# Six PSUM banks for sums and one buffer for scores, in a fused attention and gated feed-forward kernel

## The chip, the core and the metric

The kernel runs on one core of a Trainium2 chip. The metric is the device time in microseconds; the kernel before takes 428.95 us, the median of 3 runs (428.2 to 429.21). The profile is that of one execution, with a span of 426.9 us.

The engines are named as in the profile: PE is TensorE's matmul, PEld its weight load, DVE is VectorE, ACT is ScalarE, POOL is GpSimd (here it issues loads), SP is SyncE (here it issues stores and transposing transfers).

## The reference

Eight batches of twelve heads, 448 positions, 64 numbers a head. Attention squares the relu of the scores in place of a softmax; its output goes through a feed-forward block with a gate.

```python
batch, n_heads, seq, head_dim = (8, 12, 448, 64)
scores = q @ k.T / sqrt(head_dim)
attn = np.maximum(scores, 0.0) ** 2 / seq
x = (attn @ v)                      # heads side by side: 3584 x 768
g = x @ w_gate                      # 768 x 1536
gelu = 0.5 * g * (1.0 + erf(g / sqrt(2)))
val = x @ w_val                     # 768 x 1536
out = (gelu * val) @ w_out          # 1536 x 768
```

## The kernel before

All matmuls are bf16 and use a quarter of the array: 64 rows by 64 columns. The program speaks of two row halves, `PE0` (lower, rows 0 to 63) and `PE1` (upper, rows 64 to 127). Both columns of a half get one matmul each at the same time, and both halves work side by side. A line of the profile that names L159 is one of these matmuls, whichever part of the kernel it serves; the tiles tell them apart: `sp` are scores, `ff` are sums.

PSUM is shared out in two pools. A score buffer takes two banks, one for each row half; a sum takes one.

```python
    SB = 2
    FB = 4
    ...
    psS = ctx.enter_context(tc.tile_pool(name="psS", bufs=SB, space=bass.MemoryType.PSUM))
    psF = ctx.enter_context(tc.tile_pool(name="psF", bufs=FB, space=bass.MemoryType.PSUM))
```

**Sums.** There are three kinds, and all take turns in the four banks: gate and value sums (`ff<-xT,wg`, `ff<-xT,wv`; 6 steps in each half, of two matmuls of 448 columns), output sums (`ff<-wo,uT`; 12 steps in each half, 384 columns), and value products of the attention (`ff<-attnT,v`). The lower half does its steps first, then the upper half adds its own to the same bank, while the lower half is at the next sum. `wait_lower` makes the upper half wait for the last matmul of the lower.

```python
    def add_gate_value(at, b, fc, g):
        ...
        def emit(r, dc):
            if not box:
                box[0] = new_bank(done)
            if r == 1 and dc == 0:
                wait_lower(box)
            for j in range(2):
                ins = mm(box[0][HALF[j], 0:S], w[HALF[r], dc, o + P * j:o + P * (j + 1)],
                         xT[b][HALF[r], dc, :], r, j, r == 0 and dc == 0, r == 1 and dc == KC - 1)
            box[1] = ins
        ...
        ops = [[Op(f"PE{r}", GS, lambda r=r, dc=dc: emit(r, dc),
                   [w12_op[i][g], x_op[b, dc], *(ring_dep() if r == 0 and dc == 0 else ())], lag=0.24)
                for dc in range(KC)] for r in range(2)]
```

A bank is free again when its reader is done: for a gate sum the gelu on ScalarE (`gel`), for a value sum the product on VectorE (`uT`), for an output sum the copy on ScalarE (`osb`), for an attention product the copy on VectorE (`xT`). `ring` holds the readers, and `ring_dep` names the one of four sums ago.

```python
    def ring_dep():
        return [ring[-FB]] if len(ring) >= FB else []
```

**Scores.** A batch has 21 score units. A unit is a pair of matmuls in each half (of 448 columns; the units at a group's middle take two pairs of 224); its relu on ScalarE reads both banks at once (128 x 896), and VectorE squares the result. `units` holds the relus, and a unit waits for the one of two units ago.

```python
        have = [*have, *units[-SB:1 - SB]]
        ops = [[Op(f"PE{j}", 0.095 if tail else 0.189, lambda j=j, pr=pr: emit(j, pr), have, lag=0.24)
                for pr in prs] for j in range(2)]
        ...
        relu = Op("ACT", 0.8, emit_relu, [ops[0][-1], ops[1][-1], *sq_list[-4:-3]], lag=0.18, prio=2)
        ...
        units.append(relu)
```

**The planner.** The kernel decides the order of all instructions while it is built. `run_plan` takes the queues with assumed costs (the second argument of `Op`) and lags and emits, again and again, the operation that can start first. The lower half's order is fixed beforehand: the operations are sorted by their place `at`, which spreads a batch's 21 score units evenly over the feed-forward work of the batch before. The upper half's operations stand in a pool from which the planner takes what is ready.

The batches overlap: while batch b's gate, value and output sums run, the scores and the attention products of a later batch are put between them. The first two batches' queries and keys are transposed on TensorE (the second one's through the score buffers), later ones by transfers.

Of the kernel before, what the change touches and what calls it, by code (L numbers as in the profile page):

```python
# [88 lines left out]
def kernel(  # L89
# [11 lines left out]
    f32 = mybir.dt.float32  # L101
    bf16 = mybir.dt.bfloat16
# [3 lines left out]
    B, H, S, D = q.shape  # L106
# [30 lines left out]
    apool = ctx.enter_context(tc.tile_pool(name="apool", bufs=12))  # L137
    gpool = ctx.enter_context(tc.tile_pool(name="gpool", bufs=3))
    opool = ctx.enter_context(tc.tile_pool(name="opool", bufs=4))
    psS = ctx.enter_context(tc.tile_pool(name="psS", bufs=SB, space=bass.MemoryType.PSUM))  # L140
    psF = ctx.enter_context(tc.tile_pool(name="psF", bufs=FB, space=bass.MemoryType.PSUM))

    ident = const.tile([128, 128], bf16)
# [140 lines left out]
    ring = [warm_op]  # L284

    in_bank = []

    def new_bank(reader, shape=(128, 512), dtype=f32):
        in_bank.append(reader)
        return psF.tile(list(shape), dtype, name="ff", tag="F")  # L290

    def fill(t0, t1):

# [12 lines left out]
    def ring_dep():  # L306
        return [ring[-FB]] if len(ring) >= FB else []
# [14 lines left out]

    att, xT, last_s = {}, {}, {}
    t_op, relu_op, sq_op, o_op, x_op = {}, {}, {}, {}, {}
    units = []

    def add_transposes(at, b, m, rs):

        box = {}

        def emit(r):
            if b == 0:
                t = new_bank(t_op[b, m, r], [128, SC, 2 * P], bf16)
            else:
                if not box:
                    box["S"] = psS.tile([128, 2, 1024], bf16, name="sp", tag="S")
                t = box["S"][:, r, 0:SC * 2 * P].rearrange("d (c x) -> d c x", c=SC)
            box[r] = t
            src = qk16[b].rearrange("p (h c d) -> p h c d", c=SC, d=D)
            for c in range(SC):  # L340
                for j in range(2):
                    nc.tensor.transpose(t[HALF[j], c, :], src[:, 2 * (2 * m + r) + j, c, :],  # L342
                                        ident[:, :], tile_position=(0, P * j))

        def emit_copy(r):
            nc.vector.tensor_copy(by_group(qkT_tile(b))[:, m, :, r, :], box[r])

        last = units[-SB:1 - SB]
        for r in rs:
            have = [*(head_op[b, 2 * m + r, i] for i in range(2)), *(last if b else ring_dep())]  # L350
            lo = Op("PE0", 0.5, lambda r=r: emit(r), have, lag=0.2)
            hi = Op("PE1", 0.4, lambda: None)
            hi.after = lo
            t = t_op[b, m, r] = Op("DVE", 0.54, lambda r=r: emit_copy(r),
                                   [lo, last_s.get(b - 2)], lag=0.2, prio=1)
            DVE.append(t)
            if not b:
                ring.append(t)
            both(at, [(lo, hi)])
        if b:  # L360
            units.append(t)

    def add_scores(at, b, u):


        m, w = divmod(u, SC)
        tail = w == VC - 1
        prs = (2 * m, 2 * m + 1) if tail else (2 * m + (w > VC - 1),)
        cl = w if w < VC else w - VC
        box = {}  # L370

        def emit(j, pr):
            if not box:
                box[0] = psS.tile([128, 2, 512], f32, name="sp", tag="S")
            sp = box[0]
            t = by_group(qkT_tile(b))[HALF[j], m, :, pr % 2, :]
            for i in range(2):
                if tail:
                    n0 = (pr % 2) * S // 2
                    qs = t[:, :, i * P // 2:(i + 1) * P // 2]  # L380
                    mm(sp[HALF[i], j, n0:n0 + S // 2].rearrange("k (c p) -> k c p", c=SC),
                       t[:, VC - 1, HALF[1]], qs, j, i, True, True)
                else:
                    mm(sp[HALF[i], j, 0:S].rearrange("k (c p) -> k c p", c=SC),
                       t[:, cl + i * VC, HALF[1]], t[:, :, HALF[0]], j, i, True, True)

        def emit_relu():
            rl = box[1] = rpool.tile([128, 2, S], bf16, name="rl", tag="rl")
            nc.scalar.activation(rl[:, :, :], box[0][:, :, 0:S], AF.Relu)  # L389

        def emit_sq():
            a = apool.tile([128, 2, S], bf16, name="attnT", tag="attnT")
            for pr in prs:
                att[b, pr, VC - 1 if tail else cl] = a
            nc.vector.tensor_tensor(a[:, :, :], box[1][:, :, :], box[1][:, :, :], op=ALU.mult)  # L395

        if b < EARLY:
            have = [t_op[b, m, pr % 2] for pr in prs]
        else:
            have = tr_op[b, m]  # L400
        have = [*have, *units[-SB:1 - SB]]
        ops = [[Op(f"PE{j}", 0.095 if tail else 0.189, lambda j=j, pr=pr: emit(j, pr), have, lag=0.24)
                for pr in prs] for j in range(2)]
        last_s[b] = ops[1][-1]
        relu = Op("ACT", 0.8, emit_relu, [ops[0][-1], ops[1][-1], *sq_list[-4:-3]], lag=0.18, prio=2)
        n_a = len(sq_list)
        sq = Op("DVE", 0.54, emit_sq, [relu, *att_free[n_a - 12:n_a - 11]] if n_a >= 12 else [relu],
                lag=0.2, prio=2)
        units.append(relu)
        sq_list.append(sq)  # L410
        att_free.append(None)
        for pr in prs:
            sq_op.setdefault((b, pr), []).append((sq, n_a))
            sq_of[b, pr, VC - 1 if tail else cl] = sq
        ACT.append(relu)
        DVE.append(sq)
        both(at, zip(*ops))
# [3 lines left out]
    def add_values(at, b, pr):  # L421
        box = {}

        order = ([0, 3, 1, 2] if pr % 2 else [0, 1, 2, 3], [3, 0, 1, 2])
        last = (b, pr) == (0, NPAIR - 1)

        def emit(i, w):
            if pr == 0 and i == 0 and w == 0:
                xT[b] = xpool.tile([128, KC, S], bf16, name="xT", tag="xT")
            if not box:  # L430
                box[0] = new_bank(x_op[b, pr])
            if (i, w) == (1, VC - 1) or last and (i, w) == (0, 1):
                wait_lower(box)
            for j in range(2):
                o = box[0][HALF[j], 0:S]
                a = att[b, pr, w][HALF[i], j, :]
                if w < VC - 1:
                    ins = mm(o, v16[b][HALF[i], 2 * pr + j, w + i, :], a, i, j,
                       i == 0 and w == 0, i == 1 - last and w == VC - 2)
                else:  # L440
                    ins = mm(o.rearrange("d (c p) -> d c p", c=SC)[:, :, i * P // 2:(i + 1) * P // 2],
                       v16[b][HALF[i], 2 * pr + j, (1 - i) * (VC - 1), :],
                       a[:, (pr % 2) * S // 2:(pr % 2 + 1) * S // 2].rearrange(
                           "k (c p) -> k c p", c=SC), i, j, False, False)
            box[1] = ins

        def emit_copy():
# [2 lines left out]
        sqs = sq_op[b, pr]  # L450
        have = [head_op[b, pr, 2], head_op[b, pr, 3]]
        ops = [[Op(f"PE{i}", 0.189 if w < VC - 1 else 0.095, lambda i=i, w=w: emit(i, w),
                   [*have, sq_of[b, pr, w], *(ring_dep() if i == 0 else ())], lag=0.24)
                for w in order[i]]
               for i in range(2)]
        o_op[b, pr] = ops[1 - last][-1]
# [1 line left out]
            att_free[n_a] = o_op[b, pr]  # L458
        x_op[b, pr] = Op("DVE", 0.54, emit_copy, [o_op[b, pr]], lag=0.2, prio=1)
        DVE.append(x_op[b, pr])  # L460
        ring.append(x_op[b, pr])
        if last:
            ops[1][0].after = ops[0][1]
            for o, p in zip(ops[1], ops[1][1:]):
# [15 lines left out]
    def add_gate_value(at, b, fc, g):  # L480

        i, o = divmod(fc * 128, WCH)
        w = (wg, wv)[g][i]
        box = {}

        def emit(r, dc):
            if not box:
                box[0] = new_bank(done)
            if r == 1 and dc == 0:
                wait_lower(box)  # L490
            for j in range(2):
# [8 lines left out]
        def emit_mult():  # L500
            if fc == 0:
# [2 lines left out]
                uT[b][:, fc, :], gel.pop((b, fc))[:, :], box[0][:, 0:S], op=ALU.mult).ins  # L504

        ops = [[Op(f"PE{r}", GS, lambda r=r, dc=dc: emit(r, dc),
                   [w12_op[i][g], x_op[b, dc], *(ring_dep() if r == 0 and dc == 0 else ())], lag=0.24)
                for dc in range(KC)] for r in range(2)]
        if g == 0:
            done = gel_op[b, fc] = Op("ACT", 0.55, emit_gelu, [ops[1][-1]], lag=0.06, prio=0)  # L510
# [1 line left out]
        else:  # L512
# [3 lines left out]
            if b + 2 < B and b:  # L516
# [7 lines left out]
                elif fc > 6:  # L524
                    h0 = 2 * (fc - 7)
                    load_v(b + 2, h0, h0 + 4, [done])
        ring.append(done)
        if (b, fc) == (0, 0):
            at = [PLACE5 - 0.5 + 0.1 * g] * 3 + [0.01 * g] * 3
        then(at, GS, *ops, done)  # L530
# [1 line left out]
    def add_out(at, t, g):  # L532

        box = {}
        last = 2 * t + 2 == B * SC
        bounds = (0, OGS, OGS + OGS // 2, 2 * OGS) if last else (0, OGS, 2 * OGS)
        cols = slice(bounds[g], bounds[g + 1])
# [3 lines left out]

        def emit(r, fc):
            if not box:
                box[0] = new_bank(cp)
            i, o = divmod(fc, WOG)
            if r == 1 and fc == 0:
                wait_lower(box)
# [11 lines left out]
        def emit_store(j, engine, cols):  # L559
# [3 lines left out]

        ops = [[Op(f"PE{r}", step, lambda r=r, fc=fc: emit(r, fc),
                   [wo_op[fc // WOG], *(u_op[b, fc] for b, _ in chunks),
                    *(ring_dep() if r == 0 and fc == 0 else ())], lag=0.24)
                for fc in range(FC)] for r in range(2)]

        cp = Op("DVE" if last else "ACT", 0.48, emit_copy, [ops[1][-1]], prio=1)
        ring.append(cp)  # L570
        (DVE if last else ACT).append(cp)
        if t == 0:
            load_qk(2, g, H - 4, H, [cp])
# [98 lines left out]


    def emit_filler():
        t = psS.tile([128, 2, 512], f32, name="sp", tag="S")
        for _ in range(2):
            mm(t[HALF[0], 0, 0:P], warm[HALF[0], 0:P], warm[HALF[0], 0:P], 0, 0, True, True)
            mm(t[HALF[1], 0, 0:P], warm[HALF[0], 0:P], warm[HALF[0], 0:P], 0, 1, True, True)
# [68 lines left out]
```

## Time and profile before

| what | from | value |
|---|---|---|
| time, median of 3 | runs | 428.95 us |
| span of the profiled execution | page | 426.9 us |
| one relu of a score unit, 128 x 896 | groups, x168 | 918 ns |
| one gelu, 128 x 448 | groups, x96 | 543 ns |
| one copy of an output sum, 128 x 384, ACT | groups, x54 | 476 ns |
| one product into `uT`, 128 x 448, DVE | groups, x96 | 620 ns |
| one copy into `xT`, 128 x 448, DVE | groups, x48 | 624 ns |
| busy from 167.11 to 266.20 us (99.09 us): DVE, ACT | windows | 53.14, 55.71 us |

The page gives busy time per engine, then the chain of work that ended last, then the costliest groups of instructions with the mean duration of one. The windows give the same busy times for any stretch, with the number of instructions in brackets. The timeline gives the instructions of one engine in order of time, with the start, the length and, in square brackets, the idle time before them. Two things must be kept in mind. The matmuls of four tiles overlap, so PE's busy time is that of their union. And the ends of matmuls are modelled, so their starts are what can be measured.

### The profile page before, as it was taken

To read this page: it belongs to the slowest core of one execution; us is meant where nothing else is said; L and a number is where in the kernel's file an instruction comes from. 1 tells how busy PE (TensorE), PEld (TensorE's weight loads), DVE (VectorE), ACT (ScalarE), POOL (GpSimd) and SP (SyncE) were. 2 spreads that over 40 slices of the span, in tenths; PEclk is the share of its full clock that TensorE was granted. 3 is DMA by queue.
4 is the path that set the end of the run, shared out by engine and by line. 5 is a ranking of instruction groups with operands and counts; after the bars stand their busy time and mean duration, and the time that the engine had idled before them with its cause. 6 is when DMAs were issued, how large, how long until landed. Compare 5 with 4: busy or idle time off the path is not lost.

```text
span 426.9 us, 19600 instructions
## 1 busy us (share of the span) xinstructions
PE 419.6 (98%) x9090; PEld 357.1 (84%) x9090; DVE 212.9 (50%) x347; ACT 223.8 (52%) x320; POOL 73.6 (17%) x120
## 2 busy tenths in 40 slices
PE   8999999989999999999999999999999999999996
PEld 3558769767998889889999988979999988977895
DVE  3976765357643665346643666446643555212201
ACT  4956663466656555555556565555546555322220
POOL 8655401313100131012300122011310000000000
PEclk9999999999999999999999999999999999999999
DMA  7999998999983389545975379645984100120034
GB/s 101 193 199 198 200 209 128 204 128 113 118 137 81 47 114 117 125 76 89 129 121 111 46 96 144 131 63 57 139 141 96 38 4 3 46 71 3 2 77 114
DMA packets 75281, 44.91 MB, mean 105 GB/s; under 512 B 36160, under 2 KB 71744, under 8 KB 75200
## 3 DMA queue, kind: packets, MB, share of 16 engines
q0 software_dynamic: 37152, 24.39, 43.3%
q1 hardware_dynamic: 37888, 19.08, 25.0%
q8 instruction: 71, 1.16, 1.1%
q10 hardware_dynamic: 160, 0.20, 0.1%
q14 instruction: 10, 0.08, 0.1%
HBM read 48.76 MB, written 11.01 MB: 140 GB/s over the span
## 4 chain that ended last, share of the span: by engine, by line
PE 80%; DMA 13%; issue 5%; POOL 1%; DVE 0%; POOLq 0%; DVEq 0%
PE ff L159 74%; PE sp L159 6%; DMA wg<-in_moe_w_gate_dram 4%; DMA wo<-in_moe_w_out_dram 3%; DMA qk<-in_k_dram 3%; DMA qk<-in_q_dram 3%; POOL qk L211 1%; DVE uT L503 0%; POOL v L224 0%; DVE osb L557 0%; POOL ident masks.py:199 0%; POOL ident masks.py:197 0%; DVE qkr L258 0%; POOLq L211 0%; DVEq L258 0%
## 5 line engine op out<-in xcount | busy, mean ns | idle before, releaser
L159 PE MATMUL ff<-xT,wv 64*64 64x448 bf16 x2304 | 216.9, 349 | 1.6 <-issue 1.5
L159 PE MATMUL ff<-xT,wg 64*64 64x448 bf16 x2304 | 217.2, 349 | 0.1
L389 ACT ACTIVATE rl<-sp 128x896 bf16<-128x896 f32 x168 | 152.3, 918 | 97.7 <-PE sp L159 77.2
L159 PE MATMUL ff<-wo,uT 64*64 64x384 bf16 (+1 forms) x2736 | 150.6, 320 | 0.0
L159 PEld LDWEIGHTS <-wv 64*64 64x64 bf16 x2304 | 124.7, 107 | 19.2 <-issue 3.7
L159 PEld LDWEIGHTS <-wg 64*64 64x64 bf16 x2304 | 124.5, 107 | 17.6 <-issue 0.7
L395 DVE TENSOR_TENSOR attnT<-rl 128x896 bf16<-128x896 bf16 x168 | 103.8, 622 | 69.6 <-ACT rl L389 68.3
L159 PEld LDWEIGHTS <-uT 64*64 64x64 bf16 x2736 | 126.8, 107 | 4.4 <-issue 0.3
L159 PE MATMUL sp<-qkT 64*64 64x448 bf16 (+1 forms) x768 | 108.7, 328 | 0.2 <-ACT rl L389 0.2
L503 DVE TENSOR_TENSOR uT<-gel,ff 128x448 bf16<-128x448 bf16 x96 | 59.5, 620 | 73.5 <-PE ff L159 64.6
L159 PE MATMUL ff<-attnT,v 64*64 64x448 bf16 (+1 forms) x768 | 86.1, 326 | 0.1
L498 ACT ACTIVATE gel<-ff 128x448 bf16<-128x448 f32 x96 | 52.1, 543 | 51.7 <-PE ff L159 50.5
L159 PEld LDWEIGHTS <-qkT 64*64 64x64 bf16 x768 | 43.6, 106 | 10.4 <-issue 3.4
L159 PEld LDWEIGHTS <-v 64*64 64x64 bf16 x768 | 45.9, 107 | 5.8 <-issue 1.2
L557 ACT COPY osb<-ff 128x384 f32<-128x384 f32 x54 | 25.7, 476 | 45.6 <-PE ff L159 43.0
L448 DVE TENSOR_SCALAR xT<-ff 128x448 bf16<-128x448 f32 x48 | 29.9, 624 | 33.1 <-PE ff L159 33.1
L211 POOL DMA_DIRECT2D qk<-in_q_dram x25 | 15.5, 621 | 127.6 <-DVE uT L503 106.2
L224 POOL DMA_DIRECT2D v<-in_v_dram x48 | 29.5, 621 | 41.8 <-DVE uT L503 33.0
L211 POOL DMA_DIRECT2D qk<-in_k_dram x25 | 15.4, 615 | 62.2 <-DVE uT L503 54.8
L258 DVE COPY qkr<-qk 128x1792 bf16<-128x1792 bf16 x18 | 19.4, 1079 | 6.6 <-DMA qk<-in_k_dram 6.6
L557 DVE COPY osb<-ff 128x192 f32<-128x192 f32 (+1 forms) x3 | 1.2, 421 | 18.3 <-PE ff L159 18.3
L342 PEld LDWEIGHTS <-qk 128*64 128x64 bf16 x168 | 5.2, 112 | 2.9 <-issue 2.9
(23 smaller groups left out, 42.9 us busy)
## 6 DMA issues: line engine op xcount, KB each, us to landing
out_dram<-osb SPq DMA_DIRECT2D x54, 192.0 KB, 2.8
v<-in_v_dram POOLq DMA_DIRECT2D x48, 128.0 KB, 4.8
qk<-in_q_dram POOLq DMA_DIRECT2D x23, 224.0 KB, 4.5
qk<-in_k_dram POOLq DMA_DIRECT2D x23, 224.0 KB, 4.9
wg<-in_moe_w_gate_dram POOLq DMA_DIRECT2D x6, 384.0 KB, 10.5
wv<-in_moe_w_val_dram POOLq DMA_DIRECT2D x6, 384.0 KB, 11.2
wo<-in_moe_w_out_dram POOLq DMA_DIRECT2D x4, 576.0 KB, 15.3
qkT<-qkr SPq DMA_TRANSPOSE x36, 4.6
```

Source lines behind the costliest of these rows:

```text
L159: return nc.tensor.matmul(o, lhsT, rhs, start=start, stop=stop, tile_position=(P * row, P * col))
L211: op = load(4 * (h1 - h0) * S * D, lambda: nc.gpsimd.dma_start(tile_of().rearrange("p (h x) -> p h x", h=H)[:, h0:h1, :], src[b, h0:h1].re ...
L224: return nc.gpsimd.dma_start(v16[b][HALF[i], h0:h1, :, :], v[b, h0:h1].rearrange("h (p c) d -> p h c d", c=SC)[:, :, c0:c0 + VC, :])
L258: nc.vector.tensor_copy(qkr[b][:, m], qk16[b].rearrange("p (h c d) -> p c h d", c=SC, d=D)[:, :, 4 * m:4 * m + 4])
L342: nc.tensor.transpose(t[HALF[j], c, :], src[:, 2 * (2 * m + r) + j, c, :], ident[:, :], tile_position=(0, P * j))
L389: nc.scalar.activation(rl[:, :, :], box[0][:, :, 0:S], AF.Relu)
L395: nc.vector.tensor_tensor(a[:, :, :], box[1][:, :, :], box[1][:, :, :], op=ALU.mult)
L448: nc.vector.tensor_scalar_mul(xT[b][:, pr, :], box[0][:, 0:S], scalar1=out_scale)
L498: nc.scalar.activation(gel[b, fc][:, :], box[0][:, 0:S], AF.Gelu)
L503: u_op[b, fc].ins = nc.vector.tensor_tensor(uT[b][:, fc, :], gel.pop((b, fc))[:, :], box[0][:, 0:S], op=ALU.mult).ins
L557: cp.ins = (nc.vector.tensor_copy if last else nc.scalar.copy)(osb[t][:, cols], box[0][:, 0:N]).ins
```

## The change

From the end of batch 1's scores on (the second batch), the second score buffer is no longer used for scores: its two banks serve two more sums. All later scores use the one remaining buffer and wait for the relu just before. The sums then take turns in six banks: four in the old pool, then two in the halves of the former score buffer. It is for letting the lower half start a sum without waiting for a bank's reader.

The score pool is split into two pools of one buffer each; `wide` counts the sums since the change of use; `next_bank` says which bank a sum gets and for whom it waits; `next_scores` does so for a score unit.

```diff
-    psS = ctx.enter_context(tc.tile_pool(name="psS", bufs=SB, space=bass.MemoryType.PSUM))
+    psS = [ctx.enter_context(tc.tile_pool(name=f"psS{i}", bufs=1, space=bass.MemoryType.PSUM))
+           for i in range(SB)]
...
-    def new_bank(reader, shape=(128, 512), dtype=f32):
+    units, wide, spare, spare_tile = [], [], [[]], []
+
+    def new_bank(reader, shape=(128, 512), dtype=f32, half=None):
+        if half is not None:
+            if half == 0:
+                spare_tile[:] = [psS[1].tile([128, 2, 512], f32, name="ff", tag="S")]
+            return spare_tile[0][:, half, :]
         in_bank.append(reader)
         return psF.tile(list(shape), dtype, name="ff", tag="F")
+
+    def next_bank():
+
+        n = wide[0] % (FB + 2) - FB if wide else -1
+        if wide:
+            wide[0] += 1
+        if n < 0:
+            return None, ring_dep()
+        if n == 0:
+            spare.append([])
+        return n, spare[-2] if n == 0 else []
+
+    def bank_read(half, reader):
+        (ring if half is None else spare[-1]).append(reader)
+
+    def next_scores():
+
+        if wide:
+            return 0, units[-1:]
+        n = len(units)
+        return n % SB, units[n - SB:n - SB + 1]
+
+    def scores_read(n, reader):
+        units.append(reader)
+        if n == 1:
+            spare[0] = [reader]
...
-        have = [*have, *units[-SB:1 - SB]]
+        have = [*have, *free]
...
-        units.append(relu)
+        scores_read(n, relu)
+        if (b, u) == (EARLY - 1, NU - 1):
+            wide.append(0)
...   (in add_values, add_gate_value and add_out alike)
+        half, free = next_bank()
...
-                box[0] = new_bank(done)
+                box[0] = new_bank(done, half=half)
...
-                   [w12_op[i][g], x_op[b, dc], *(ring_dep() if r == 0 and dc == 0 else ())], lag=0.24)
+                   [w12_op[i][g], x_op[b, dc], *(free if r == 0 and dc == 0 else ())], lag=0.24)
...
-        ring.append(done)
+        bank_read(half, done)
```

More of the change, by code (lines that the diff above doesn't have):

```diff
@@ L324 @@
     t_op, relu_op, sq_op, o_op, x_op = {}, {}, {}, {}, {}
-    units = []
     def add_transposes(at, b, m, rs):
@@ L335, in emit @@
                 if not box:
-                    box["S"] = psS.tile([128, 2, 1024], bf16, name="sp", tag="S")
+                    box["S"] = psS[n].tile([128, 2, 1024], bf16, name="sp", tag="S")
                 t = box["S"][:, r, 0:SC * 2 * P].rearrange("d (c x) -> d c x", c=SC)
@@ L346, in emit_copy @@
             nc.vector.tensor_copy(by_group(qkT_tile(b))[:, m, :, r, :], box[r])
-        last = units[-SB:1 - SB]
+        n, last = next_scores() if b else (0, [])
         for r in rs:
@@ L360, in add_transposes @@
         if b:
-            units.append(t)
+            scores_read(n, t)
     def add_scores(at, b, u):
@@ L370, in add_scores @@
         box = {}
+        n, free = next_scores()
         def emit(j, pr):
             if not box:
-                box[0] = psS.tile([128, 2, 512], f32, name="sp", tag="S")
+                box[0] = psS[n].tile([128, 2, 512], f32, name="sp", tag="S")
             sp = box[0]
@@ L430, in emit @@
             if not box:
-                box[0] = new_bank(x_op[b, pr])
+                box[0] = new_bank(x_op[b, pr], half=half)
             if (i, w) == (1, VC - 1) or last and (i, w) == (0, 1):
@@ L452, in add_values @@
         ops = [[Op(f"PE{i}", 0.189 if w < VC - 1 else 0.095, lambda i=i, w=w: emit(i, w),
-                   [*have, sq_of[b, pr, w], *(ring_dep() if i == 0 else ())], lag=0.24)
+                   [*have, sq_of[b, pr, w], *(free if i == 0 else ())], lag=0.24)
                 for w in order[i]]
@@ L460, in add_values @@
         DVE.append(x_op[b, pr])
-        ring.append(x_op[b, pr])
+        bank_read(half, x_op[b, pr])
         if last:
@@ L484, in add_gate_value @@
         box = {}
+        half, free = next_bank()
         def emit(r, dc):
             if not box:
-                box[0] = new_bank(done)
+                box[0] = new_bank(done, half=half)
             if r == 1 and dc == 0:
@@ L534, in add_out @@
         box = {}
+        half, free = next_bank()
         last = 2 * t + 2 == B * SC
@@ L543, in emit @@
             if not box:
-                box[0] = new_bank(cp)
+                box[0] = new_bank(cp, half=half)
             i, o = divmod(fc, WOG)
@@ L565, in add_out @@
                    [wo_op[fc // WOG], *(u_op[b, fc] for b, _ in chunks),
-                    *(ring_dep() if r == 0 and fc == 0 else ())], lag=0.24)
+                    *(free if r == 0 and fc == 0 else ())], lag=0.24)
                 for fc in range(FC)] for r in range(2)]
         cp = Op("DVE" if last else "ACT", 0.48, emit_copy, [ops[1][-1]], prio=1)
-        ring.append(cp)
+        bank_read(half, cp)
         (DVE if last else ACT).append(cp)
@@ L674, in emit_filler @@
     def emit_filler():
-        t = psS.tile([128, 2, 512], f32, name="sp", tag="S")
+        t = psS[0].tile([128, 2, 512], f32, name="sp", tag="S")
         for _ in range(2):
```

## The prediction

> **What bounds the kernel now.** I read the busy shares first, then the engine's waits, then the chain, then short stretches of it.
>
> The busy shares on the page of the kernel before:
> ```profile
> PE 419.6 (98%) x9090; PEld 357.1 (84%) x9090; DVE 212.9 (50%) x347; ACT 223.8 (52%) x320; POOL 73.6 (17%) x120
> ...
> PEclk9999999999999999999999999999999999999999
> ```
> TensorE is the engine to look at: VectorE and ScalarE are half idle and the clock is full throughout. But "98%" is only a union of matmuls whose ends are modelled. Four 64x64 tiles work side by side, so PE counts as busy when one of its two row halves stands still.
>
> The chain of waits, in order of time (start, length, what):
> ```profile
> 3.13 1.74 POOL qk L211 x3
> ...
> 41.96 13.87 DMA wo<-in_moe_w_out_dram
> 55.88 14.44 issue
> ...
> 167.11 1.95 PE ff L159 x48
> ...
> 266.20 1.95 PE ff L159 x48
> ...
> 365.07 55.63 PE ff L159 x1253
> ```
> Up to about 95 us the chain runs through loads and issue; after that through matmuls alone. The same piece returns at 167.11, 266.20 and 365.07: the steady state repeats every two batches, in 99.1 and 98.9 us.
>
> What would two batches take without a wait? A 448-column matmul of one half follows the one before after 0.189 us, a 384-column one after 0.1625 (from the rule named below; starts in the timeline are 0.19 and 0.16 apart). Per half: 48 gate and value sums x 6 x 0.189 = 54.5; 7 output tiles x 2 sums x 12 x 0.1625 = 27.3; 42 score units, 8.0; 12 value products of the attention, 8.0. Sum 97.7. So **1.2 to 1.4 us per two batches, 0.6 to 0.7 per batch, are lost**; that is all a bank can win in the steady state.
>
> Where? Busy time and count of records in three stretches (stretch; length; PE, PEld, DVE, ACT, POOL busy; clock; DMA):
> ```profile
> 179.65:180.10 0.45, 0.45 (x10) 0.10 (x2) 0.37 (x1) 0.45 (x3) 0.00 (x0) 1.00 0.00 0
> 210.80:211.45 0.65, 0.65 (x16) 0.55 (x12) 0.56 (x1) 0.51 (x1) 0.00 (x0) 1.00 1.27 204
> 386.00:394.00 8.00, 8.00 (x177) 6.08 (x169) 1.86 (x3) 2.17 (x4) 0.00 (x0) 1.00 0.01 2
> ```
> A record counts in every stretch that it touches and lasts 0.35 us. At full rate one expects (length + 0.35) x 4 / 0.189: 177 in the third (there are 177), but 17 in the first, where there are 10. The second, of 384 columns (0.32 us each), should have 24 and has 16. In both, PE is "busy" and one half is idle. ScalarE around the first of them:
> ```profile
> 178.78 0.92 ACT L389 ACTIVATE rl<-sp 128x896 bf16<-128x896 f32 x1 [1.15 <-PE sp L159]
> 179.59 0.47 ACT L557 COPY osb<-ff 128x384 f32<-128x384 f32 x1
> 179.95 0.56 ACT L498 ACTIVATE gel<-ff 128x448 bf16<-128x448 f32 x1
> ```
> The lower half's next value sum starts at 180.12, just after the output copy leaves its bank at 179.59 + 0.47 = 180.06; that copy stood behind the relu of a score unit. This is a wait for a bank.
>
> I put each matmul's start beside the program's order and added up, per row half, the time beyond 0.189 or 0.1625 since the previous start. From 100 to 420 us the lower half idles 4.2 us, the upper 4.8. The pattern repeats: the upper half idles about 0.65 where a batch's gate stage turns into output sums (164, 211, 263, 310, 362 us: 0.63, 0.67, 0.63, 0.67, 0.6), and the lower idles 0.4 to 0.5 where outputs turn into gates (137, 180, 236, 279), with smaller waits after. The reason: a sum's lower pass runs ahead of its upper one. An output pass lasts 12 x 0.1625 = 1.95, a gate pass 1.13. Into the outputs, the upper half finishes its short pass 0.8 before the lower finishes a long one. Back into gates, the lower half should keep that lead, but has no fifth bank, and loses it again.
>
> **What the Trainium skill says.** "PSUM — Partial Sum Buffer", Specifications: 8 banks of 512 fp32 values; two score buffers of two banks and four sum banks use all, so the change can only re-divide them. No view shows banks. "TensorEngine Tiling (Array Packing)", Gotcha 1: different row tiles can't access the same bank at once; hence the upper pass waits for the lower, and the 210.80 stretch agrees. "TensorE: Matmul & The Clock Gate", Back-to-back issue gap: N/2.4 + 2.5 ns, so 189.2 and 162.5; the 177 records of 177 agree. "Perfetto Trace Analysis", Optimization Strategy: a gap that repeats on the engine that should be saturated can mean too little PSUM; the repeating 0.4 to 0.5 us agrees.
>
> **The change, part by part.** No instruction is added or removed: 9090 matmuls, the same relus and copies. Only the order and what each waits for change, and only after batch 1's scores, about 65 us in.
>
> *Six banks for sums.* I took the order of both programs and computed the lower half's lead over the upper, in matmul time put in the queue (medians over 1.2 us). Lowest lead in six gate stages (batches 1 to 6) and highest in the output stage after each:
> - before: 1.18 to 1.97, 1.23 to 2.17, 1.13 to 2.02, 1.23 to 2.17, 1.23 to 2.36, 1.99 to 2.36. Rises: 0.79 + 0.94 + 0.89 + 0.94 + 1.13 + 0.37 = 5.1.
> - after: 1.89 to 2.19, 1.97 to 2.36, 1.89 to 2.19, 1.97 to 2.36, 1.78 to 2.36, 2.32 to 2.36. Rises: 0.30 + 0.39 + 0.30 + 0.39 + 0.58 + 0.04 = 2.0.
>
> Each rise is time in which the upper half stands still. With batch 0's (0.75 and 0.85) the totals are about 5.8 and 2.9: the order saves 2.9. Before, the order said 5.8 and the trace has 4.8, a ratio of 0.83; so I expect **2.4 us** back.
>
> *One buffer for scores.* A unit now holds the only buffer from its first matmul until its relu is done: 0.38 (both halves together), 0.2 to the relu's start (80.44 to 81.04, then 81.25 in one early unit), 0.92 of relu: 1.5 us. If a gelu (0.54) or an output copy (0.48) stands ahead, 2.0. In the order after, units stand 1.9 to 2.9 us of matmul time apart from batch 3 on; mostly enough, but in gate stages the upper half comes later (unit length 0.75 to 0.94), leaving 0 to 0.4 us. In batch 2's scores (80 to 125 us) they stand only 1.5 to 2.4 apart, where a gelu in the way is a wait of 0.1 to 0.3. Some 21 dense units, a few of them hit: I put **0.4 us** on this, all of it on the path, since each half takes its matmuls in order.
>
> *Moved work.* The two halves of a score unit, up to 3.9 us of matmul time apart before, now come almost together. ScalarE and VectorE get another order of the same work, at about 55% of their time: hidden.
>
> Sum: -2.4 + 0.4 = -2.0, and 428.95 - 2.0 = **426.9 us**.
>
> **Rivals.**
> 1. *The score wait takes the place of the bank wait.* For it: the 1.5 to 2.0 us loop against 1.9 apart; two buffers let the upper half do scores early where it would idle, and that filling is lost. Against: ScalarE is 52% busy, and the planner, which knows of the single buffer, spaces the units. At 0.1 us for each of 126 units, 12 us, the result would be 439; at 0.1 for one in five, the gain is gone: 429.
> 2. *The lower half only runs further ahead and nothing comes back.* The end is set by the upper half's last sums. For it: the last output sums end with the upper half alone. Against: the upper half's backlog fills exactly its idle 0.65 at the next outputs. It would leave 428.9.
> 3. *All bank and transition waits vanish* and the new one costs nothing: at most 4.2 us, 424.8.
> 4. *ScalarE becomes the bound.* 55.7 us of 99 per two batches speak against it.
>
> **Range and chances.** The most that the idle time allows is 4.2, and it needs rival 3; a score wait of 0.1 in one unit of five costs 2.5 and, with the 2.4, gives 429.0. Between these the range is 425.0 to 429.3. A gain of over 2% would be 8.6 us, twice the idle time that there is: 0.01. A loss of 8.6 us needs rival 1 nearly at full: 0.02. Within 2%: 0.97.
>
> **What would show each step.** Two-batch period in the chain: from 99.0 to about 98.3. Records in a 0.45 us stretch where outputs turn into gates: about 17 in place of 10. Upper half's idle time at the second and later turns into outputs: 0.3 in place of 0.65; the first turn (110 to 115 us) unchanged. Everything before 65 us unchanged. Wrong if matmuls of scores wait for the relu again and again (idle lower half ahead of "sp" matmuls, in the batch 2 stretch above all), or if the lower half still waits for copies at the turns.

## The result and the profile after

The changed kernel takes **460.13 us** against 429.08 of the kernel before in the same runs: a ratio of 1.0742 (95% interval 1.0701 to 1.0782). The prediction was 426.9, with a range of 425.0 to 429.3. The 31 us have one cause, and it was not among the rivals.

Its page, the lines on busy time and clock:

```profile
PE 426.3 (93%) x9090; PEld 351.9 (77%) x9090; DVE 213.2 (47%) x347; ACT 224.3 (49%) x320; POOL 73.6 (16%) x120
...
PEclk9999999999999999999999999999999999999999
```

The counts of instructions are those of the kernel before on all five engines, and the clock is full. PE's share fell from 98% to 93%, so now there are moments when both halves stand still.

Who waited for whom on PE (line waited for; us in total, times, longest). The view counts only time in which the whole array is empty:

```profile
PE ff L160 <- DVE uT L539: 11.2, 18, 0.8
PE ff L160 <- DVE xT L483: 7.5, 11, 0.7
PE ff L160 <- ACT gel L534: 4.3, 7, 0.7
PE ff L160 <- ACT osb L594: 1.4, 3, 0.6
...
PE sp L160 <- ACT rl L421: 0.2, 1, 0.2
```

The same view of the kernel before has, for matmuls of sums on readers of sums, one line:

```profile
PE ff L159 <- DVE uT L503: 0.2, 1, 0.2
```

There are 39 waits of matmuls of *sums* (`ff`) for *readers of sums*, 0.6 us of empty array each, and they are spread over all four kinds of reader. Scores (`sp`) left the array empty for a relu once, for 0.2 us. A score that holds up only the lower half is not in this view; for it the starts of the matmuls were put beside the program's order. From 100 to 420 us the lower half stands still ahead of scores 13 times without a stop of the upper half beside it. Each of these stops is of 0.31 us or less and ends some 0.05 us after a relu; together they are 2.3 us. So rival 1, scores waiting for the one buffer, is there, but far too small for 31 us.

The chain of waits, in order of time, near the end, where no attention is left:

```profile
408.54 0.63 DVE uT L539
409.17 0.04 issue
409.21 7.01 PE ff L160 x142
...
416.31 0.63 DVE uT L539
416.95 0.04 issue
416.99 7.01 PE ff L160 x142
...
424.09 0.63 DVE uT L539
424.73 0.04 issue
424.77 6.96 PE ff L160 x143
```

Before, this stage lay in one piece of 55.63 us of matmuls. Now a product on VectorE cuts it every 7.78 us. Six gate and value sums take 6 x 1.13 = 6.8 us; with a stall of 0.97 that makes 7.8. **Here the stall comes once in each turn through the six banks**, and it comes without any scores nearby.

One of them in the timeline (start, length, engine, instruction, idle time before and what ended it):

```profile
415.48 0.73 PE L160 MATMUL ff<-xT,wg 64*64 64x448 bf16 x10
416.31 0.62 DVE L539 TENSOR_TENSOR uT<-gel,ff 128x448 bf16<-128x448 bf16 x1 [2.03 <-PE ff L160]
416.99 0.94 PE L160 MATMUL ff<-xT,wg 64*64 64x448 bf16 x14 [0.78 <-DVE uT L539]
```

And the stretch of it (stretch; length; PE, PEld, DVE, ACT, POOL busy; clock; DMA):

```profile
416.10:416.95 0.85, 0.11 (x4) 0.00 (x0) 0.62 (x1) 0.00 (x0) 0.00 (x0) 1.00 0.00 0
```

The matmuls that start at 416.99 are those of a gate sum. Their bank was taken long before, and the data they read were there; yet they wait for the product that reads the value sum *before* them. By the starts and the program's order, that is the pair in the two halves of the former score buffer: the value sum in the first half (last matmul started at 415.48) and the gate sum in the second (first upper steps at 415.64 and 415.83, the third only at 416.99).

The changed kernel takes both halves from one tile of 128 x 2 x 512. The semaphores are set while the kernel is built, from the tiles that each instruction touches, in the order in which the planner emits them. To that bookkeeping the two sums are one object. The product on VectorE was emitted after the second upper step of the gate sum, and in the built program it waits for that step; the third step comes after the product, and waits for the product. Neither needs the other: they are different banks. In the built program 41 upper-half matmuls of sums carry a wait for ScalarE or VectorE, against 2 before. The 39 new ones are the stalls: in front of them the upper half stands still for 34.4 us in all, 0.88 each.

### The profile page after: what moved, and what is told of

Its sections match the earlier page's. It is cut to its first block, busy times and chain, and to the rows that moved or that the text cites. A ratio compares the mean times of both kernels' runs of the same rounds, so it can differ in the third digit from the quotient of the medians.

```text
span 456.7 us, 19664 instructions
## 1 busy us (share of the span) xinstructions
PE 426.3 (93%) x9090; PEld 351.9 (77%) x9090; DVE 213.2 (47%) x347; ACT 224.3 (49%) x320; POOL 73.6 (16%) x120
## 4 chain that ended last, share of the span: by engine, by line
PE 90%; DVE 5%; ACT 2%; DMA 2%; issue 1%; SPq 0%; DVEq 0%; ACTq 0%
PE ff L160 79%; PE sp L160 8%; DVE uT L539 3%; DMA qkT<-qkr 2%; DVE xT L483 2%; PE ff L336 1%; PE ff L748 1%; ACT gel L534 1%; PE ff L373 1%; PE sp L373 1%; ACT osb L594 0%; ACT rl L421 0%; SPq L599 0%; DVE attnT L427 0%; DVE qkr L259 0%
## 5 line engine op out<-in xcount | busy, mean ns | idle before, releaser
L160 PE MATMUL ff<-xT,wg 64*64 64x448 bf16 x2304 | 197.9, 350 | 12.0 <-DVE uT L539 9.9
L160 PE MATMUL ff<-xT,wv 64*64 64x448 bf16 x2304 | 194.5, 349 | 6.5 <-ACT gel L534 4.3
L160 PE MATMUL ff<-wo,uT 64*64 64x384 bf16 (+1 forms) x2736 | 154.4, 320 | 6.1 <-DVE xT L483 3.3
L160 PEld LDWEIGHTS <-wg 64*64 64x64 bf16 x2304 | 115.2, 107 | 33.8 <-issue 18.3
L160 PEld LDWEIGHTS <-uT 64*64 64x64 bf16 x2736 | 120.4, 107 | 18.3 <-issue 9.9
L160 PEld LDWEIGHTS <-wv 64*64 64x64 bf16 x2304 | 116.0, 107 | 23.9 <-issue 10.0
L160 PE MATMUL sp<-qkT 64*64 64x448 bf16 (+1 forms) x768 | 105.8, 328 | 0.5 <-DMA qkT<-qkr 0.3
L160 PE MATMUL ff<-attnT,v 64*64 64x448 bf16 (+1 forms) x768 | 88.4, 326 | 0.1
L160 PEld LDWEIGHTS <-qkT 64*64 64x64 bf16 x768 | 45.0, 106 | 11.6 <-issue 4.3
```

The lines of the kernel that those rows point to most:

```text
L160: return nc.tensor.matmul(o, lhsT, rhs, start=start, stop=stop, tile_position=(P * row, P * col))
```

## The experiments

Theory A: the waits between the two sums of one tile are the whole loss. Theory B: the one score buffer is (rival 1 of the prediction). Theory C: the new order of the matmuls is. Each run is compared with the kernel before on the same chip.

### One score buffer alone, and five or six banks without a shared tile

`four`: no sum goes to the former score buffer.

```diff
-        n = wide[0] % (FB + 2) - FB if wide else -1
-        if wide:
-            wide[0] += 1
+        n = -1
```

> One score buffer from the end of batch 1's scores on, sums in the four old banks, the other score buffer left unused. Theory A (two sums in the halves of one tile: a matmul of the second sum waits for the reader of the first): 428.5 to 431, the wait of scores for the one buffer being small. Theory B (the one score buffer makes scores wait for relus): 450 to 460, as the changed kernel. Theory C (the new order of the matmuls, with the lower half 1.9 to 2.4 us ahead, costs the time): 428.5 to 431, for this order swings as that of before does.

`five`: only its first half is used.

```diff
-        n = wide[0] % (FB + 2) - FB if wide else -1
+        n = wide[0] % (FB + 1) - FB if wide else -1
```

> One score buffer; sums in five banks, only the first half of the former score buffer is used, so no tile holds two sums. The order of all 9090 matmuls is the same as in the changed kernel. Theory A: 426 to 428, and no stalls of 0.9 us of both halves. Theory B: 450 to 460. Theory C: 455 to 460.

`six`: both banks are used, as two tiles. The pool of the second score buffer is closed at the change of use, and one with two tiles takes its place; each bank then waits for its own last reader.

```diff
...
-            if half == 0:
-                spare_tile[:] = [psS[1].tile([128, 2, 512], f32, name="ff", tag="S")]
-            return spare_tile[0][:, half, :]
+            if not psX:
+                late.close()
+                psX.append(late.enter_context(
+                    tc.tile_pool(name="psX", bufs=1, space=bass.MemoryType.PSUM)))
+            return psX[0].tile(list(shape), dtype, name="ff", tag=f"X{half}")
...
-        if n == 0:
-            spare.append([])
-        return n, spare[-2] if n == 0 else []
+        spare[n].append([])
+        return n, spare[n][-2]
...
```

> One score buffer; sums in six banks as in the changed kernel, but the two late banks are two tiles of their own in place of the halves of one tile. The order of all 9090 matmuls is again the same. Theory A: as with five banks, 426 to 428. Theory B: 450 to 460. Theory C: 455 to 460.

| run | time, us | before, us | ratio (95% interval) |
|---|---|---|---|
| four | 428.77 | 428.39 | 1.0009 (0.9997 to 1.0020) |
| five | 425.80 | 428.39 | 0.9941 (0.9925 to 0.9958) |
| six | 425.91 | 428.39 | 0.9952 (0.9934 to 0.9970) |

B falls: with one score buffer and nothing else the kernel is 0.4 us from the one before, and the interval takes in no difference at all. C falls too, and more sharply: in `five` and `six` the order of all 9090 matmuls is that of the changed kernel, to the last one, and they are 34 us faster than it. What differs is which tile a sum stands in, and with it the waits: in both, 2 upper-half matmuls of sums wait for ScalarE or VectorE, as before the change. Both came in 0.1 to 0.2 us below the 426 that theory A allowed. And the intended change, freed of the shared tile, **is 2.5 us faster than the kernel before** by the medians, 2.1 by the ratio (1.3 to 2.8).

In the waits on PE of `six` no sum waits for a reader any more; beside the start, transfers and issue this is left:

```profile
PE sp L162 <- ACT rl L424: 0.5, 2, 0.3
```

The chain of `six`: the piece that came back after 99.1 us before (and after 108.9 in the changed kernel, 223.85 and 332.78) comes back after 309.16 - 210.98 = 98.2:

```profile
210.98 1.95 PE ff L162 x48
...
309.16 1.95 PE ff L162 x48
...
361.79 55.18 PE ff L162 x1251
```

The two stretches of the prediction, in `six` at the same turns (outputs into gates, then gates into outputs):

```profile
177.95:178.40 0.45, 0.45 (x17) 0.45 (x12) 0.00 (x0) 0.45 (x1) 0.00 (x0) 1.00 0.00 0
208.65:209.30 0.65, 0.65 (x21) 0.62 (x16) 0.23 (x1) 0.00 (x0) 0.00 (x0) 1.00 1.10 110
```

17 records where there were 10, which is the full rate: the lower half no longer waits for a bank. 21 in place of 16 at the other turn, where 24 would be full.

### The waits put back by hand

If A is right, `six` with the waits of the changed kernel added must lose the 31 us again, though no two sums share a tile. The waits can also be added one by one.

```diff
+    def pair_mm(half, box):          # after each step of a sum
+        if half is None:             # not in a late bank
+            return
+        p = box["p"]                 # shared by the two sums of a turn
+        r = p.pop(("read", 1 - half), None)
+        if UPPER_WAITS and r is not None:
+            tc.add_manual_dep(recent[-2].ins, r.ins.name, SYNC, reason="pair")
+        p["mm", half] = recent[-1]
+
+    def pair_read(half, box, ins):   # at the reader of a sum
+        if half is not None:
+            p = box["p"]
+            p["read", half] = ins
+            if READER_WAITS and ("mm", 1 - half) in p:
+                tc.add_manual_dep(ins.ins, p["mm", 1 - half].ins.name, SYNC, reason="pair")
+        return ins
...
```

`w_both` has both kinds of wait (and 41 waiting upper-half matmuls, as the changed kernel), `w_upper` only the first, `w_reader` only the second.

> Six banks in tiles of their own, with the changed kernel's waits put back by hand: a matmul of one late bank waits for the reader of the other one where that reader stands ahead of it in the order, and a reader waits for the other bank's last matmul ahead of it. The data do not need these waits. Theory A (the waits between the two sums of one tile are the whole loss): 457 to 461, with some 36 stalls of 0.9 us. Theory A' (the shared tile costs in another way, by its place in PSUM or its release): 425 to 430.

> As before, but only the matmul's wait for the other bank's reader. Theory A: the reader now starts 0.46 us after its own bank's last matmul start, not 0.83, so each stall is some 0.6 us in place of 0.97; 39 of them: 446 to 452. Theory A': 425 to 430.

> As before, but only the reader's wait for the other bank's last matmul. It comes up to 0.4 us later, and with six banks nobody waits for it: 425 to 427 under theory A. If late readers are what costs (they feed the next products and the release of banks): over 430.

| run | time, us | before, us | ratio (95% interval) |
|---|---|---|---|
| w_both | 459.27 | 427.96 | 1.0727 (1.0703 to 1.0752) |
| w_upper | 447.20 | 427.96 | 1.0445 (1.0392 to 1.0497) |
| w_reader | 426.09 | 427.96 | 0.9952 (0.9934 to 0.9971) |

All three fall where theory A put them. The whole loss comes back within the intervals (1.0727 here, 1.0742 for the changed kernel), so nothing else about the shared tile costs anything that shows. The waits on PE, `w_both` first:

```profile
PE ff L165 <- DVE uT L571: 11.3, 18, 0.8
PE ff L165 <- DVE xT L511: 7.5, 11, 0.7
```

then `w_upper`:

```profile
PE ff L165 <- DVE uT L571: 5.8, 18, 0.5
PE ff L165 <- DVE xT L511: 3.2, 10, 0.4
```

The same 18 waits are half as long. Here is why. In the changed kernel the product on VectorE of a value sum in a bank of its own starts 0.46 us after that sum's last matmul started, here after 410.94:

```profile
411.40 0.62 DVE L539 TENSOR_TENSOR uT<-gel,ff 128x448 bf16<-128x448 bf16 x1 [2.24 <-PE ff L160]
```

In the pair it started 0.83 after (416.31 after 415.48), that is 0.45 after the neighbour's second step (415.86), for which it had to wait. Alone this delay costs nothing that shows (`w_reader`), since with six banks nobody is waiting for the bank. But where a matmul waits for the reader, it lengthens that wait. In front of the 39 waiting matmuls the upper half stands still for 34.4 us in the changed kernel, 0.88 each, and for 20.5 us in `w_upper`, 0.53 each. The times say the same: the changed kernel is 34.2 us above `six`, `w_upper` 21.3.

### The planner told of the wait

`told` is the changed kernel with its shared tile, and one more dependency in the plan (in the three kinds of sums alike):

```diff
+        if half == 1:
+            ops[1][0].deps += spare[-1][:1]
```

> The changed kernel with its shared tile, but the planner is told that the upper pass of the tile's second sum waits for the first sum's reader, and can put other upper passes ahead of it. Theory A, loss by an order that does not know of the wait: 426 to 434. If the wait can't be filled, since the upper half has nothing else that is ready: 445 to 460.

It takes 444.63 us against 427.96 (1.0386; 1.0338 to 1.0434): between the two expectations, 0.4 us short of the second. Half of the loss is recovered. Of the waits of sums for readers one is left in the view:

```profile
PE ff L160 <- DVE xT L483: 0.7, 1, 0.7
```

In front of the matmuls that carry such a wait the upper half now stands still for 5.0 us in all, in place of 34.4. But the lower half still idles 15.9 us between 100 and 420 us (30.9 in the changed kernel), 8.5 of them ahead of scores that start 0.05 us after a relu; ten of these stops last 0.4 to 0.9 us. The planner puts other work of the upper half ahead, and the score units seem to hold their one buffer longer for it; that last step is argued from the waits and was not tried by itself.

### Two attempts at a better version

`early` is `six` with the change of use one batch earlier; `six_relu` is `six` with the planner reckoning 0.92 us for a relu in place of 0.8.

```diff
-        if (b, u) == (EARLY - 1, NU - 1):     # early
+        if (b, u) == (0, NU - 1):
...
-        relu = Op("ACT", 0.8, emit_relu,      # six_relu
+        relu = Op("ACT", 0.92, emit_relu,
```

> Six banks in tiles of their own, and the change of use already after batch 0's scores. Batch 1's scores and its transposes, which stand close together (some 1.7 us apart), then use one buffer as well. If one score buffer costs little even there: 425 to 426.5. If the close stretch is where it costs, since relu, copy and the next unit must follow one another: 428 to 434, with scores waiting for the relu or the transposes' copy between 25 and 65 us.

> Six banks in tiles of their own; the planner reckons with 0.92 us for a relu, as measured, in place of 0.8. Six stalls of 0.15 to 0.19 us ahead of scores are left in the version with six tiles, 1 us in all; if the planner's short relu makes them: 425 to 425.7. If they come from the even spacing of the units: 425.6 to 426.3, no difference from it.

`early` takes 427.86 against 428.28 (0.9993; 0.9977 to 1.0008): the gain of `six` is gone, and the time is 0.1 us short of the second expectation. Its last long piece of matmuls begins 3.2 us after that of `six` (361.79):

```profile
365.00 55.18 PE ff L162 x1251
```

Between 25 and 70 us gaps of over 0.1 us in its lower half sum to 5.8 us, those of `six` to 2.3. The three longest ahead of scores and transposes, 1.35, 1.02 and 0.56 us, end 0.05 to 0.07 us after a relu, as the second expectation said. So in a close stretch one score buffer does cost, about 2 us. `six_relu` takes 426.19 against 428.28 (0.9950; 0.9920 to 0.9980), which is `six` again: between 100 and 420 us its lower half stands still ahead of scores for 2.0 us, that of `six` for 1.8. The planner's short relu is not what makes these waits. The best versions remain `five` and `six`, which can't be told apart.

## Why the prediction was wrong

- **The failed step** stands at the head of "The change, part by part": only order and waits change, and then these waits were reckoned by bank, as if a sum waited for the reader of its own bank alone and a score unit for its own buffer alone. I read from the code who should wait for whom (`spare`, `free`) and not from the built program who does. Missing from the sum is one term: 39 waits of a sum for the reader of its neighbour in the tile, 0.88 us each in which the upper half idles, and with it soon the lower: 34.4 us, where 460.13 - 425.91 is 34.2. It could be read beforehand: the waits of the built program show it, 41 against 2, and the diff has one `tile([128, 2, 512])` for two sums.
- *Six banks, -2.4.* Right in mechanism and about right in size once the tiles are apart. `four` and `six` both have one score buffer and differ in the banks: 428.77 - 425.91 = 2.9, or 2.4 by their ratios. From 100 to 420 us the upper half's idle time fell from 4.8 to 2.2 and the lower half's from 4.2 to 1.7. At the later turns into outputs the upper half's stop, counted as the one gap at the turn, fell from 0.49 to 0.59 us before to 0.15 to 0.26: by about 0.34, where 0.35 was expected (0.65 to 0.3), though both ends lie lower. The two-batch period is 98.2 (98.3). The sixth bank was not needed: `five` does the same.
- *One buffer for scores, +0.4.* `four` measures it beside four banks: 428.77 - 428.39 = 0.4 (-0.1 to 0.9 by the interval). With six banks it is not where I put most of it, and there is more of it. In `six` nearly all that is left of the lower half's idle time from 100 to 420 us stands ahead of scores that wait for a relu: 16 stops of up to 0.22 us, spread over all batches, against 0.35 us in `four` and none in the kernel before. What they cost in time was not separated. So the forecast gain of 2.0, against 2.1 to 2.5 measured, may owe something to luck: the lower half won back nearly all of its 4.2 us, and lost part of that to the scores.
- *Rival 1* named the right direction and even a time of 439, but by the wrong wait. Its sign, an idle lower half ahead of `sp` matmuls, is there with 2.3 us. *Rivals 2 and 4* are refuted by `six` and by ScalarE's 49%; *rival 3* was too hopeful.
- *The chances.* 0.02 for over 2% slower was far too little. The 4.2 us of idle time bounded the gain. Nothing bounded the loss, for a change that gives every sum a new partner in the bookkeeping of waits.
- The Trainium skill's page "TensorEngine Tiling (Array Packing)", Gotcha 1, leaves it to software to synchronize row tiles that share a bank. Here software also set waits between two different banks, which that page does not ask for, and they cost the 31 us.

## What to carry to other kernels

In this program a tile is the unit in which waits are kept: two independent sums in one tile wait for each other, even in different banks. When a buffer is given a second use, allocate it in the pieces in which it will be written and read, then compare the waits of the built program, engine by engine, with those meant. A stall that comes once per turn of a ring of buffers, with a length that fits a reader's duration, points at such a wait.

## What the runs showed of the hardware

A wait of one half soon stopped the other as well. In the stretch from 416.10 to 416.95 only four records touch PE, though the lower half had begun a sum at 415.48 and its next step carries no wait. That step stands just behind the waiting matmul of the upper half in the program's order, and started with it, at 417.00. From 100 to 420 us the change raised the idle time of the upper half from 4.8 to 31.9 us and that of the lower from 4.2 to 30.9. And a reader's late start by itself was free here: in `w_reader` products on VectorE start up to 0.93 us after their sum's last matmul in place of 0.46, and its ratio to the kernel before is that of `six`, 0.9952.
